# Turning q and k of six batches by crossbar DMA instead of on TensorE, with q copied by ScalarE in its own row order and k by VectorE in blocks

## The chip, the cores and the metric

The kernel runs on one core of a Trainium2 chip. The metric is the time of one execution on the device in microseconds. Executions whose time lies more than 1.5% above the fastest of the same kernel are put down as slow and left out of the ratios. A profile is one execution; its span is some 2 us shorter than the time. The granted clock is the share of TensorE's full clock that the profile records. In this kernel TensorE's results go to PSUM tiles and the other tiles lie in SBUF; a crossbar transpose (`dma_start_transpose`) is a transfer that turns a tile on its way, here from SBUF to SBUF.

## The reference

Attention over a sliding window with a bias by distance (8 batches, 8 heads, 576 rows of 64), then two matrix products with ELU between them, for 4608 tokens:

```python
rel = pos[:, None] - pos[None, :]
bias = slopes[:, None, None] * (-np.abs(rel))[None]
scores = np.where((rel >= 0) & (rel < 128), q @ k^T / 8 + bias, -1e9)
x = softmax(scores) @ v                  # then heads side by side: 4608 x 512
h = x @ w_in                             # 512 -> 2048
out = np.where(h > 0, h, np.exp(np.minimum(h, 0)) - 1) @ w_out   # 2048 -> 512
```

## The kernel before

Work is laid out in steps of about 2.1 us, 16 to a batch. In each step TensorE makes one tile of the hidden layer (`hp`), one tile of scores (`sp`), one of values (`av`) and a quarter of an output tile (`op`), each for a different stage. ScalarE takes the exponentials (`e`, `EX`) and copies finished outputs (`ob`). GpSimd clips `e`; VectorE makes `g` from `e` and `hp` (which frees the buffer of `hp`), masks `EX` and normalizes. A step s may also carry tasks, written `at(s, task)`, and the order in the program is the order on each engine.

Scores need q and k with the head's 64 dimensions on the partitions, so both are turned. A load puts rows 4p to 4p+3 of a head on partition p, so a turned tile has every fourth row side by side. The kernel before leaves q and k in that order, 32 columns to a block, and undoes it in the stores:

```python
QK = [one([128, H, 2, 640], F16, f"QK{i}") for i in range(2)]      # q and k of one batch
ps_s = ctx.enter_context(tc.tile_pool(name="ps_s", bufs=2, space=PSUM))
# ...
def load_v(b, n):                        # SyncE, four issues a block of 128 rows
    # ...
    for j in range(4):
        nc.sync.dma_start(t[32 * j:32 * j + 32, :, :],
                          v[b, :, 128 * n + j:128 * n + 128:4, :].rearrange("h p d -> p h d"))

def transposes(b, hp):                   # two heads, q and k: eight 128x128 on TensorE
    t = ps_s.tile([128, 2, 2, 4, 2, 32], F16, name="tp", tag="sps")
    # ... eight nc.tensor.transpose ...
    for odd in range(2):                 # q and k together, neighbours in runs of 32
        r = slice(64 * odd, 64 * odd + 64)
        o = QK[b % 2][0:64, 2 * hp:2 * hp + 2, :, 0:512].rearrange(
            "p h w (n a i) -> p (h w) n a i", a=2, i=32)[:, :, :, odd, :]
        i = t[r, :, :, :, :, :].rearrange("p h w n a i -> p (h w) (n a) i")
        if hp % 2:
            nc.scalar.copy(o, i)
        else:
            V.tensor_copy(o, i)
# ...
for hp in range(NP):
    at(s0 + ((5, 9, 10, 13) if b > 1 else (9, 10, 13, 14) if b else (14, 14, 15, 15))[hp],
       transposes, b + 1, hp)
# ...
for p0, rows in rows_of(512 * t + 128 * ts):          # stores of every fourth row
    nc.sync.dma_start(rows, ob[p0:p0 + rows.shape[0], :])
```

The scores share the two PSUM buffers `sps` with these turned tiles. SyncE's queue issues v's loads, the stores, and the crossbar transposes of the normalized rows (`xT<-xn`) from batch 2 on. GpSimd issues the loads of q and k.

The softmax here doesn't subtract the row's maximum and nothing guards it: scores larger than these inputs give would overflow.

## Time and profile before

| | before |
|---|---|
| time, median of 3 (lowest to highest) | 367.59 us (366.04 to 368.22) |
| span of the profile, mean clock | 363.7 us, 0.995 |
| TensorE, VectorE, ScalarE, GpSimd busy | 340.3, 243.5, 206.7, 145.7 us |
| batches 0 to 7, first step to first step (batch 0 from its step 4, the first that makes a tile of the hidden layer) | 33.4, 42.0, 38.6, 37.9, 36.8, 36.7, 36.8, 33.7 us |
| end phase, from the last batch's end to the end of the span | 51.1 us |

The views that show what bounds it are in the prediction. These are the groups on the page that the change replaces, and the granted clock of TensorE. A group line is: line, engine, operation, out<-in, shapes, count; then busy time in all and mean ns of one; then idle time just before and what ended most of it. The clock line has one digit for a fortieth of the span, in tenths.

```profile
PEclk9899999999999999999999999999999999999999
...
L322 ACT COPY QK<-tp 64x1024 f16<-64x1024 f16 x28 | 28.1, 1005 | 1.6 <-PE tp L312 1.4
...
L324 DVE COPY QK<-tp 64x1024 f16<-64x1024 f16 x28 | 19.2, 684 | 1.1 <-PE tp L312 0.8
L312 PE MATMUL tp<-ident,stq 128*128 128x128 f16 x224 | 17.1, 219 | 2.3 <-ACT QK L322 1.0
```

The reader sees 56 copies of 1024 elements a partition, spread over two engines.

### The profile page before, as it was taken

How to read it: one execution, taken by the hardware profiler on the slowest of the kernel's cores; microseconds unless marked ns; L12 is line 12 of the kernel's file. 1: busy time of each engine (PE TensorE's matmuls, PEld its weight loads, DVE VectorE, ACT ScalarE, POOL GpSimd, SP SyncE). 2: the span in 40 equal slices, each digit the busy share in tenths (PEclk: the TensorE clock that was granted, in tenths of full speed). 3: DMA queues.
4: the chain of work that ended last, by engine and by line, in shares of the span. 5: the costliest groups of instructions: out<-in, count | busy, mean ns of one | idle time of the engine just before them, and what ended most of it. 6: DMA issues, size and time to landing. Idle time of an engine off the chain costs nothing.

```text
span 363.7 us, 9613 instructions
## 1 busy us (share of the span) xinstructions
PE 340.3 (94%) x3790; PEld 251.6 (69%) x3790; DVE 243.5 (67%) x574; ACT 206.7 (57%) x349; POOL 145.7 (40%) x229
## 2 busy tenths in 40 slices
PE   6878997999979999989999999999999999999994
PEld 6766775777647667767777777777777777666651
DVE  6479889678886776666676767776776756634430
ACT  4355583666537655765566665666567565543431
POOL 9146623434314723472346334642433232233320
PEclk9899999999999999999999999999999999999999
DMA  8999999839243973497448934793631222211113
GB/s 114 198 206 119 228 107 183 151 80 155 38 103 89 133 108 84 110 128 110 98 94 127 127 88 100 120 136 82 102 84 45 52 47 45 51 43 47 29 43 73
DMA packets 81948, 37.06 MB, mean 102 GB/s; under 512 B 51952, under 2 KB 77296, under 8 KB 81904
## 3 DMA queue, kind: packets, MB, share of 16 engines
q0 software_dynamic: 34064, 15.40, 35.5%
q1 hardware_dynamic: 47840, 21.06, 25.6%
q8 instruction: 29, 0.48, 0.6%
q14 instruction: 15, 0.12, 0.1%
HBM read 36.70 MB, written 9.44 MB: 127 GB/s over the span
## 4 chain that ended last, share of the span: by engine, by line
PE 65%; DVE 14%; ACT 9%; DMA 7%; issue 3%; POOL 1%; SPq 0%; ACTq 0%; POOLq 0%
PE hp L451 27%; PE op L492 25%; PE sp L348 5%; ACT QK L322 5%; DVE VP L116 4%; DMA vs<-in_v_dram 3%; PE av L394 3%; DVE g L463 3%; ACT EX L372 2%; DVE QK L324 2%; ACT e L455 2%; DVE EX L380 2%; DMA xT<-xn 2%; DMA stq<-in_q_dram 1%; DVE xn L415 1%
## 5 line engine op out<-in xcount | busy, mean ns | idle before, releaser
L456 POOL TENSOR_SCALAR e<-e 128x512 f32<-128x512 f32 x144 | 88.6, 615 | 199.9 <-ACT e L455 199.9
L451 PE MATMUL hp<-xT,wi 128*128 128x256 f16 (+3 forms) x1536 | 150.3, 246 | 8.1 <-DVE g L463 3.6
L451 PEld LDWEIGHTS <-wi 128*128 128x128 f16 x1536 | 121.5, 98 | 49.9 <-DVE g L463 5.5
L455 ACT ACTIVATE e<-hp 128x512 f32<-128x512 f32 x144 | 86.0, 597 | 119.0 <-PE hp L451 110.0
L492 PE MATMUL op<-wo,g 128*128 128x512 f16 x576 | 146.4, 379 | 0.0
L463 DVE SCALAR_TENSOR_TENSOR g<-e,hp 128x512 f16<-128x512 f32 x144 | 98.0, 681 | 23.9 <-POOL e L456 22.7
L380 DVE TENSOR_TENSOR EX<-EX,band 128x512 f16<-128x512 f16 x112 | 49.8, 445 | 57.1 <-ACT EX L372 57.0
L372 ACT ACTIVATE EX<-sp 128x512 f16<-128x512 f32 x128 | 75.9, 593 | 13.3 <-PE sp L368 8.6
L492 PEld LDWEIGHTS <-g 128*128 128x128 f16 x576 | 51.2, 98 | 36.9
L348 PE MATMUL sp<-QK 128*128 128x128 f16 (+3 forms) x576 | 49.8, 213 | 0.0
L394 PE MATMUL av<-VP,EX 128*128 128x65 f16 x576 | 38.6, 193 | 4.3 <-DVE EX L380 2.7
L394 PEld LDWEIGHTS <-EX 128*128 128x128 f16 x576 | 31.6, 98 | 8.7 <-DVE EX L380 4.2
L415 DVE TENSOR_TENSOR xn<-av,rden 128x256 f16<-128x256 f32 x80 | 34.0, 424 | 2.8
L348 PEld LDWEIGHTS <-QK 128*128 128x128 f16 (+1 forms) x576 | 31.3, 97 | 1.0 <-issue 0.2
L496 ACT COPY ob<-op 128x512 f32<-128x512 f32 x36 | 21.1, 586 | 14.3 <-PE op L492 6.4
L322 ACT COPY QK<-tp 64x1024 f16<-64x1024 f16 x28 | 28.1, 1005 | 1.6 <-PE tp L312 1.4
L414 DVE RECIPROCAL rden<-av 128x4 f32<-128x4 f32 x80 | 14.4, 180 | 16.0 <-PE av L394 14.6
L134 POOL TENSOR_SCALAR VP<-vf 128x512 f16<-128x512 f32 (+1 forms) x25 | 19.5, 779 | 2.7 <-DMA vf<-in_v_dram 2.7
L324 DVE COPY QK<-tp 64x1024 f16<-64x1024 f16 x28 | 19.2, 684 | 1.1 <-PE tp L312 0.8
L312 PE MATMUL tp<-ident,stq 128*128 128x128 f16 x224 | 17.1, 219 | 2.3 <-ACT QK L322 1.0
L312 PEld LDWEIGHTS <-stq 128*128 128x128 f16 x224 | 13.8, 98 | 3.4 <-issue 3.2
L116 DVE COPY VP<-vs 32x512 f16<-32x512 f16 x48 | 14.9, 310 | 1.3 <-DMA vs<-in_v_dram 0.5
(70 smaller groups left out, 118.5 us busy)
## 6 DMA issues: line engine op xcount, KB each, us to landing
out_dram<-ob SPq DMA_DIRECT2D x128, 64.0 KB, 1.7
vf<-in_v_dram SPq DMA_DIRECT2D x80, 64.0 KB, 2.3
stq<-in_k_dram POOLq DMA_DIRECT2D x7, 512.0 KB, 6.4
stq<-in_q_dram POOLq DMA_DIRECT2D x7, 512.0 KB, 7.5
wi<-in_moe_w_in_dram POOLq DMA_DIRECT2D x4, 512.0 KB, 13.8
wo<-in_moe_w_out_dram POOLq DMA_DIRECT2D x4, 512.0 KB, 15.1
QK<-TQ SPq DMA_DIRECT2D x2, 576.0 KB, 8.0
vs<-in_v_dram POOLq DMA_DIRECT2D x2, 512.0 KB, 9.9
```

Source lines behind the costliest of these rows:

```text
L312: nc.tensor.transpose(t[:, g, w, :, j, :], stq[b][:, w, 2 * hp + g, 2 * j:2 * j + 2, :].rearrange("p a d -> p (a d)"), ident)
L322: nc.scalar.copy(o, i)
L348: nc.tensor.matmul(t[:, o:o + n], qk[0:r, h, 1, kc:kc + 128], qk[0:r, h, 0, qc:qc + n], start=b > 0 or o == 0, stop=b > 0)
L372: nc.scalar.activation(e[:, 0:512], t, AF.Exp, scale=0.125)
L380: V.tensor_tensor(out=e, in0=e, in1=band[:, c:c + n].unsqueeze(1).broadcast_to([128, 512 // n, n]), op=ALU.min)
L394: nc.tensor.matmul(a[:, l, :], e[:, c:c + 128], vp[:, n, h, 0:D + 1], start=st, stop=sp)
L415: V.tensor_tensor(out=xnt[b, i][:, 4 * half:4 * half + 4, :], in0=a[:, :, 0:D], in1=r.unsqueeze(2).broadcast_to([128, 4, D]), op=ALU.mult)
L451: nc.tensor.matmul(p[:, l * w + u0:l * w + u1], w_in_sb[:, c, fc * 128:(fc + 1) * 128], xT[:, c, x0:x0 + u1 - u0], start=(c == 0), stop=(c ...
L455: nc.scalar.activation(e, p, AF.Exp)
L456: nc.gpsimd.tensor_scalar(out=e, in0=e, scalar1=1.0, scalar2=0.0, op0=ALU.min, op1=ALU.max)
L463: V.scalar_tensor_tensor(out=gs[t][:, f0:f0 + nf, c0:c0 + w], in0=sh(es.pop((t, j))), scalar=1.0, in1=sh(hps.pop((t, j))), op0=ALU.subtrac ...
L492: nc.tensor.matmul(ops[t], gs[t][:, fc, ts * 128:(ts + 1) * 128], w_out_sb[:, fc, :], start=(fc == 0), stop=(fc == NFC - 1))
```

## The change

The intent is to take the transposes of batches 2 to 7 from the engine that bounds the kernel. The crossbar's output `tq` is a tile in SBUF, so it takes none of the scores' PSUM buffers. ScalarE then puts q in its own row order, by writing every fourth element, so that the output rows come in order and each store is one issue. VectorE leaves k in blocks. q and k get tiles of their own. In batches 0 and 1 TensorE still turns, but there too ScalarE copies q and VectorE copies k.

```diff
-    QK = [one([128, H, 2, 640], F16, f"QK{i}") for i in range(2)]
+    QT = [one([128, H, 576], F16, f"QT{i}") for i in range(2)]
+    KT = [one([128, H, 640], F16, f"KT{i}") for i in range(2)]
 # ... the constant rows and masks: a second set for q in its own order ...
+        def put(t, b, w, hs, c0, n):                 # batches 0 and 1, out of PSUM
+            for odd in range(2):
+                i = t[64 * odd:64 * odd + 64].rearrange("p h n a i -> p h n a i", i=32)
+                if w:
+                    # ... k: V.tensor_copy in runs of 32 ...
+                else:
+                    o = QT[b % 2][0:64, hs, c0:c0 + n].rearrange(
+                        "p h (n i a o) -> p h n a i o", a=2, o=2, i=32)[:, :, :, :, :, odd]
+                    nc.scalar.copy(o, i)
+        def cross(b, n):
+            w, hp = n // NP, n % NP
+            # ...
+            nc.sync.dma_start_transpose(
+                out=tq[b][:, w, 2 * hp:2 * hp + 2, :, :].rearrange("p h a c -> p (h a) c"),
+                in_=stq[b][:, w, 2 * hp:2 * hp + 2, :, :].rearrange("p h j d -> p (h j d)"))
+        def uncross_k(b, j):
+            # ... V.tensor_copy in runs of 32 ...
+        def uncross_q(b, n):
+            hs, j = slice(4 * (n // 4), 4 * (n // 4) + 4), n % 4
+            nc.scalar.copy(QT[b % 2][0:64, hs, 0:512].rearrange("p h (c j) -> p h c j", j=4)[:, :, :, j],
+                           tq[b][64 * (j % 2):64 * (j % 2) + 64, 0, hs, j // 2, :])
 # ...
-                for p0, rows in rows_of(512 * t + 128 * ts):
-                    nc.sync.dma_start(rows, ob[p0:p0 + rows.shape[0], :])
+                nc.sync.dma_start(out[r:r + 128, :], ob)
 # ...
+                    for n in range(8):
+                        at(s0 + (n if b > 1 else 6 + n // 2), cross, b + 1, n)
+                        at(s0 + (5 + n if b > 1 else 8 + n), uncross_q, b + 1, n)
+                        if n < 4:
+                            at(s0 + (9 + n if b > 1 else 12 + n), uncross_k, b + 1, n)
 # ...
-            at(32 + n, place_v4, 2, n)
+            at(24 + 2 * n, place_v4, 2, n)
```

## The prediction

> **What bounds the kernel now.** First the page's line of busy time:
>
> ```profile
> PE 340.3 (94%) x3790; PEld 251.6 (69%) x3790; DVE 243.5 (67%) x574; ACT 206.7 (57%) x349; POOL 145.7 (40%) x229
> ```
>
> TensorE leads, but busy time alone doesn't show that it is full, so next the busy time by stretch (length; then PE, PEld, DVE, ACT, POOL; clock, DMA share, GB/s). The first stretch is set-up and batch 0, the second the end of batch 1, the third the start of batch 2, the last one period of batch 5.
>
> ```profile
> 20.00:40.00 20.00, 15.91 (x247) 12.68 (x247) 17.84 (x52) 11.38 (x18) 10.85 (x16) 1.00 1.20 163
> ...
> 70.86:92.10 21.24, 20.45 (x293) 16.12 (x292) 16.30 (x36) 13.95 (x22) 8.06 (x13) 1.00 0.77 118
> 92.10:107.45 15.35, 12.32 (x153) 8.55 (x152) 13.00 (x38) 6.86 (x12) 3.90 (x8) 1.00 0.37 71
> ...
> 190.10:226.90 36.80, 36.33 (x377) 26.70 (x376) 25.96 (x58) 23.61 (x42) 16.68 (x26) 1.00 0.66 111
> ```
>
> In batch 0 VectorE is the fullest (17.84 of 20); at the start of batch 2 again (13.00 of 15.35, TensorE 12.32); from then on TensorE (36.33 of 36.80). The chain of waits in batch 5 shows of what a step (a sixteenth of a batch) consists:
>
> ```profile
> 214.00 0.87 PE hp L451 x8
> 214.87 0.12 PE av L394 x4
> 214.99 0.22 PE sp L348 x4
> 215.21 0.86 PE op L492 x4
> 216.08 0.87 PE hp L451 x8
> 216.95 0.12 PE av L394 x4
> 217.07 0.22 PE sp L348 x4
> 217.30 0.45 PE tp L312 x8
> ```
>
> A step is 2.08 us of gapless matmuls, and eight transposes add 0.45 us. A batch has 16 steps (33.3), 0.24 for the two steps with double av, four transpose groups (1.8), the tail's transposes (0.39): 35.7. It takes 36.8, so about 1.1 us is stall. Of that about 0.6 is at the second and fourth group, whose two ScalarE copies of 1.0 us hold a scores buffer (in the chain, ACT QK L322 twice a batch). So a transpose taken from TensorE is worth its full time there.
>
> **What the Trainium skill says.** "VectorE: DVE Perf Modes", section The three transpose paths: TensorE's transpose lands in PSUM, the crossbar DMA's in SBUF, 1309 ns for 128x128. Here the existing crossbar transposes, four such blocks each, land in 2.4 us at the median. The page gives no issue time; this trace does: 1193 ns of SyncE's queue for each of 30. Same page, section The perf-mode tier table: 16-bit copies in SBUF run up to 4x, from PSUM at most 2x. The trace agrees with the direction: 684 ns for 64x1024 from PSUM, while 32x256 and 32x512 in SBUF take about 210 and 310, which extrapolates to 0.4 to 0.5 us for 64x1024 (estimate). "ScalarE: Activation LUTs", section What ACT_TABLE_LOAD costs: a copy with immediate scale takes 186 ns + 0.833 ns an element. The trace's 128x128 copy from SBUF took 294, which is that; so 512 elements give 0.61 us (estimate). No run yet shows ScalarE writing every fourth element.
>
> **The change part by part.**
> 1. Removed: 32 transposes in each of batches 2 to 7. 6 x 4 x 0.45 = 10.8 us of TensorE, in the bounding stretch. With the stalls at the ScalarE copies, up to 6 x 2.4 = 14.4.
> 2. ScalarE: 4 copies of 1.005 (4.0 us a batch) become 8 of 0.61 (4.9). One a step fits the idle of about 1.0 us that ScalarE has before each e in most steps. Hidden.
> 3. VectorE: 4 of 0.684 (2.7) become 4 of 0.45 (1.8), and the tail's 2 of 0.417 become 4 of about 0.28 (+0.3). Even.
> 4. Set-up: VectorE gains groups(1), about 1.05 us, and loses a second subtraction (0.58), pm (0.46) and a wait for posi (1.3, early); k alone goes to it in batches 0 and 1 (+0.9 together), two split tails (+0.6). About 1 us more work where VectorE bounds; against it, q's first copy no longer waits for the second transpose group in steps 14 and 15, where ScalarE idled 0.69 twice. Net 0, give or take 1.
> 5. place_v4 of batch 2 (16 copies of 0.31, 4.8 us with their issue) moves from steps 32-35 to 24-30. Steps 32-37 then need TensorE's 12.3 instead of 15.35: -3 us. But steps 24-31 get VectorE work of 16.3 + 4.8 - 2.7 + 1.8 + 0.3 = 20.5 and still take about 21, so batch 2's own transposes gain little. Together -3.3.
> 6. SyncE's queue: 136 row stores at 0.42 become 36 whole ones, but 48 crossbar transposes at 1.2 come in, eight in the first eight steps of a batch. In that half lie already the v loads (four a pair of steps) and three turns of xn. SyncE's timeline in batch 5 of the kernel before:
>
> ```profile
> 205.82 2.72 SPq L423 DMA_TRANSPOSE xT<-xn  x2
> 208.63 2.01 SPq L126 DMA_DIRECT2D vf<-in_v_dram  x4
> 212.56 2.14 SPq L498 DMA_DIRECT2D out_dram<-ob  x4
> 214.80 1.19 SPq L423 DMA_TRANSPOSE xT<-xn  x1
> 216.09 4.45 SPq L126 DMA_DIRECT2D vf<-in_v_dram  x8
> 221.33 1.38 SPq L498 DMA_DIRECT2D out_dram<-ob  x3
> 222.83 2.34 SPq L423 DMA_TRANSPOSE xT<-xn  x1
> ```
>
> Nothing follows a transpose in less than its 1.2 us, so the issue blocks the queue. Put the new order end to end, counted from the batch's first step (205.38 here). Ahead of cross 7, the last quarter of k, lie four turns of xn at 1.3 with the gap behind them (5.2), seven crosses at 1.25 (8.7), three groups of v loads at 2.05 (6.2) and two stores at 0.55 (1.1). The first turn finds its xn ready at 0.2, and after it the queue doesn't run empty: cross 7 starts at 0.2 + 5.2 + 8.7 + 6.2 + 1.1 = 21.4 and lands 2.4 later, at 23.8. VectorE reaches the first copy of k after the cut of step 9: 9 x 2.08 + 0.2 (the first step is longer) + 2.6 = 21.5. So it stands 2.3 us. Behind the copy lies the elu of step 9, which frees the buffer of the hidden tile of step 11, due at 11 x 2.08 + 0.2 = 23.1. With 0.45 for the copy and 0.65 for the elu: 23.8 + 0.45 + 0.65 - 23.1 = **1.8 us of TensorE stall per batch**. Some issues here take 1.05 more (the 2.34 above), others' gaps are shorter, so 1.2 to 2.7, 1.9 in the middle.
>
> **Sum.** Batches 2 to 6 (which turn 3 to 7): 5 x (2.4 - 1.9) = 2.5. Batch 2's start: 3.3. Set-up 0. The last store: one issue instead of four, 1.2 less, with a longer landing: 0.5. Total about 6.3: 367.6 - 6.3 = 361.3, say 361.
>
> **Rivals.**
> A. The transfers are hidden. If SyncE runs far enough ahead or the copy of k is not missed, all 2.4 us a batch stay: 5 x 2.4 + 3.3 + 0.5 = 15.8, 352 us. For it: SyncE waits 149 us in total for ob, so over a whole batch it has room (about 28 us of work in 35), and the writer put two steps between the last cross and its use. Against: the bunching above.
> B. ScalarE becomes the bound in steps 5 to 12: exp, e, a quarter of ob and the copy are 0.5 + 0.5 + 0.12 + 0.52 = 1.65 of 2.08. If writing every fourth element costs 1.0 instead of 0.61, it is 2.0 and every store step slips, about 1 us a batch: 366.
> C. DMA contention. Landings of turns beside q and k loads took 4.6 to 6.4 instead of 2.4; the crosses come before those loads, mostly beside v loads, where 2.4 to 3.6 was seen. If crosses took 5, stall grows by 2.6 a batch: 374. Also late v loads would hold GpSimd's cast, and with it e.
> D. "SBUF — State Buffer", section two separate sides: a VectorE copy in a two-port mode locks GpSimd out for its whole length. Four copies of 0.45 a batch against e's min of 0.61; TensorE copies from PSUM did not do that. At worst 1 us a batch; the casts of v (4 times 0.31 in a row) show e's min at 0.72 instead of 0.61, so less.
>
> **Range and chances.** A gives 352, B 366, both of C's ends near 370; my sum 361, which is 1.8% under the median before. The 2% line is 360.2, within the error of a stall of 1.2 to 2.7 times five (7 us). So 353.5 to 368, chances 0.46 faster, 0.48 same, 0.06 slower.
>
> **What would show it.** tp L312 falls from 224 to 32 transposes. ScalarE's new copies at 0.61 mean, VectorE's at 0.45. A wait of VectorE's first k copy on the DMA that fills tq, about 2 us in each of batches 2 to 6, and after it hidden tiles waiting for elu; SyncE without a gap from the batch's start to cross 7, about 21 us. Steps 32 to 37 in 12 us. If that wait is absent, rival A holds and I am wrong by 9 us; if copies of q take 1 us, B; if crosses land in 5, C.

## The result

The changed kernel is correct and slower: 402.81 us median of four runs (397.02 to 408.65), of which two, 397.02 and 400.44, count as fast; the kernel before took 367.9 beside it. A ratio in this document is the mean time of one kernel's fast runs over that of the other's of the same rounds, so not quite the ratio of the medians. Here it is 1.083 (95% interval 1.069 to 1.098). The other two, 405.19 and 408.65, are left out by the 1.5% rule, though their clocks (0.953 and 0.941, against 0.949 and 0.952) set them little apart; with all four the ratio would be 1.094. The profile is of the run of 400.44 us.

The page after, in the lines that answer to those of before:

```profile
PE 343.8 (86%) x3598; PEld 249.6 (63%) x3598; DVE 244.0 (61%) x601; ACT 252.7 (63%) x381; POOL 145.2 (36%) x230
...
PEclk9696988999699998999899999999996999999999
...
L353 ACT COPY QT<-tq 64x512 f16<-64x512 f16 x48 | 64.4, 1341 | 1.1
...
L345 DVE COPY KT<-tq 64x1024 f16<-64x1024 f16 x24 | 10.5, 436 | 21.7 <-DMA tq<-stq 21.3
...
L303 ACT COPY QT<-tp 64x512 f16<-64x512 f16 x12 | 15.5, 1295 | 6.0 <-DVE KT L298 5.1
```

TensorE has 192 matmuls fewer and yet 3.5 us more busy time, with its clock falling in several slices (mean 0.949). The prediction gave those transposes 10.8 us, so some 14 us more went into the rest of its work (an estimate from these numbers). VectorE's k copies take what was predicted, 436 ns, but wait 21 us for the crossbar. ScalarE's q copies take 1341 ns from SBUF and 1295 from PSUM, twice the predicted 610, and ScalarE's busy time rises by 46 us.

The time from first step to first step shows that the loss lies in every stage but the last batch, which turns nothing, and the end. Here `start` ends where step 4 of batch 0 begins.

| us | start | b0 | b1 | b2 | b3 | b4 | b5 | b6 | b7 | end |
|---|---|---|---|---|---|---|---|---|---|---|
| before | 16.7 | 33.4 | 42.0 | 38.6 | 37.9 | 36.8 | 36.7 | 36.8 | 33.7 | 51.1 |
| after | 20.0 | 39.9 | 53.0 | 41.6 | 41.9 | 40.0 | 37.1 | 41.1 | 33.7 | 50.3 |

**Batches 0 and 1.** ScalarE's timeline (start, duration, engine and line, operation, count; in brackets the idle time before and its releaser) has in steps 14 and 15 of batch 0:

```profile
51.04 5.22 ACT L303 COPY QT<-tp 64x512 f16<-64x512 f16 x4 [0.73 <-PE tp L327]
...
57.91 5.25 ACT L303 COPY QT<-tp 64x512 f16<-64x512 f16 x4 [0.53 <-DVE KT L298]
```

Before, ScalarE had two copies of 1.0 us (2.03) in each of these places. While it holds the turned tiles, the scores have no PSUM buffer. In batch 1 a second thing comes in. These lines are VectorE's, TensorE's in the step after it, and TensorE's one step later:

```profile
102.73 0.42 DVE L345 COPY KT<-tq 64x1024 f16<-64x1024 f16 x1 [7.07 <-DMA tq<-stq]
...
105.12 1.89 PE L480 MATMUL hp<-xT,wi 128*128 128x128 f16 x16 [7.07 <-DVE g L492]
...
109.13 1.06 PE L480 MATMUL hp<-xT,wi 128*128 128x128 f16 x16
```

VectorE stands at the first k copy until the last crossbar transpose has landed, 7.07 us. Behind that copy lie four copies that place v (1.18 us) and the `g` that frees a hidden buffer, so TensorE stands as long. The 16 matmuls after it take 1.89 us; the next 16, 4 us later, take 1.06.

**Batch 4**, in which the clock stayed at 1.00, can be accounted for nearly in full. Its steps of 2.1 us are longer in three places. The lines are from the timelines of ScalarE, TensorE, VectorE and GpSimd:

```profile
211.42 1.34 ACT L353 COPY QT<-tq 64x512 f16<-64x512 f16 x1
...
213.24 1.02 PE L506 MATMUL op<-wo,g 128*128 128x512 f16 x4 [0.72 <-ACT ob L510]
...
221.77 0.53 DVE L345 COPY KT<-tq 64x1024 f16<-64x1024 f16 x1 [2.58 <-DMA tq<-stq]
...
222.94 1.03 PE L480 MATMUL hp<-xT,wi 128*128 128x256 f16 x8 [2.32 <-DVE g L492]
...
228.86 0.62 POOL L136 TENSOR_SCALAR VP<-vf 128x512 f16<-128x512 f32 x1 [3.55 <-DMA vf<-in_v_dram]
...
230.82 0.69 DVE L492 SCALAR_TENSOR_TENSOR g<-e,hp 128x512 f16<-128x512 f32 x1 [2.55 <-POOL e L485]
...
231.56 1.05 PE L480 MATMUL hp<-xT,wi 128*128 128x256 f16 x8 [2.19 <-DVE g L492]
```

First, in the step with an output store, the q copy of 1.34 us delays ScalarE's `ob` copy and TensorE waits 0.7 us for it (step of 3.0 us, +0.9). Second, the k copy waits 2.58 us for the crossbar, and TensorE 2.32 for what lies behind it (+2.6). Third, v's load of 222.07 lands 6.65 us later, beside the 512 KB load of k issued at 221.13; GpSimd's cast waits 3.55 us for it and holds `e`, VectorE waits for `e`, and TensorE for VectorE, 2.19 us (+2.4). Together +5.9; the removed transposes are -2.4 by the prediction; so 36.8 becomes 40.3, and 40.0 was measured.

SyncE's queue in that batch, which starts at 196.40 (first part and last):

```profile
196.82 1.22 SPq L339 DMA_TRANSPOSE tq<-stq  x1
198.46 2.05 SPq L452 DMA_TRANSPOSE xT<-xn  x1
200.56 1.26 SPq L339 DMA_TRANSPOSE tq<-stq  x1
201.92 2.01 SPq L128 DMA_DIRECT2D vf<-in_v_dram  x4
203.97 1.19 SPq L339 DMA_TRANSPOSE tq<-stq  x1
...
219.15 1.26 SPq L339 DMA_TRANSPOSE tq<-stq  x1
220.51 2.01 SPq L128 DMA_DIRECT2D vf<-in_v_dram  x4
```

It has no gap worth naming until the last crossbar of k at 219.15, 22.75 us after the batch's start; it landed 2.49 us later.

### The profile page after: what moved, and what is told of

Same layout as the page of the kernel before. It is cut to its first block, busy times and chain, and to the rows that moved or that the text cites. A ratio compares the mean times of both kernels' runs of the same rounds, so it can differ in the third digit from the quotient of the medians.

```text
span 398.6 us, 9247 instructions
## 1 busy us (share of the span) xinstructions
PE 343.8 (86%) x3598; PEld 249.6 (63%) x3598; DVE 244.0 (61%) x601; ACT 252.7 (63%) x381; POOL 145.2 (36%) x230
## 4 chain that ended last, share of the span: by engine, by line
PE 54%; DMA 12%; ACT 12%; DVE 10%; SPq 5%; issue 5%; POOL 1%; ACTq 0%; DVEq 0%; POOLq 0%
PE hp L480 23%; PE op L506 20%; DMA tq<-stq 5%; PE sp L377 5%; DMA vf<-in_v_dram 4%; ACT QT L353 4%; ACT QT L303 3%; DVE g L492 3%; PE av L423 3%; ACT EX L401 3%; DMA xT<-xn 3%; DVE VP L118 2%; SPq L339 2%; ACT e L484 2%; SPq L452 2%
## 5 line engine op out<-in xcount | busy, mean ns | idle before, releaser
L480 PE MATMUL hp<-xT,wi 128*128 128x256 f16 (+3 forms) x1536 | 157.3, 253 | 32.7 <-DVE g L492 24.1
L480 PEld LDWEIGHTS <-wi 128*128 128x128 f16 x1536 | 126.2, 101 | 76.7 <-issue 19.1
L484 ACT ACTIVATE e<-hp 128x512 f32<-128x512 f32 x144 | 88.2, 612 | 108.9 <-PE hp L480 100.9
L506 PE MATMUL op<-wo,g 128*128 128x512 f16 x576 | 149.0, 384 | 4.0 <-ACT ob L510 4.0
L353 ACT COPY QT<-tq 64x512 f16<-64x512 f16 x48 | 64.4, 1341 | 1.1
L377 PE MATMUL sp<-QT,KT 128*128 128x128 f16 (+3 forms) x576 | 51.7, 219 | 4.5 <-ACT QT L303 4.5
L377 PEld LDWEIGHTS <-KT 128*128 128x128 f16 (+1 forms) x576 | 33.0, 100 | 5.7 <-issue 4.5
L510 ACT COPY ob<-op 128x512 f32<-128x512 f32 x36 | 22.2, 616 | 12.9 <-PE op L506 11.7
L345 DVE COPY KT<-tq 64x1024 f16<-64x1024 f16 x24 | 10.5, 436 | 21.7 <-DMA tq<-stq 21.3
L303 ACT COPY QT<-tp 64x512 f16<-64x512 f16 x12 | 15.5, 1295 | 6.0 <-DVE KT L298 5.1
L118 DVE COPY VP<-vs 32x512 f16<-32x512 f16 x48 | 16.7, 348 | 0.8
L519 PE MATMUL spare<-ident 128*128 128x128 f16 x94 | 8.9, 269 | 1.6 <-DVE ident L179 1.6
## 6 DMA issues: line engine op xcount, KB each, us to landing
wi<-in_moe_w_in_dram POOLq DMA_DIRECT2D x4, 512.0 KB, 12.3
```

The source lines that it names most:

```text
L353: nc.scalar.copy(QT[b % 2][0:64, hs, 0:512].rearrange("p h (c j) -> p h c j", j=4)[:, :, :, j], tq[b][64 * (j % 2):64 * (j % 2) + 64, 0, h ...
L377: nc.tensor.matmul(t[:, o:o + n], kt[0:r, h, kc:kc + 128], qt[0:r, h, qc:qc + n], start=b > 0 or o == 0, stop=b > 0)
L480: nc.tensor.matmul(p[:, l * w + u0:l * w + u1], w_in_sb[:, c, fc * 128:(fc + 1) * 128], xT[:, c, x0:x0 + u1 - u0], start=(c == 0), stop=(c ...
L484: nc.scalar.activation(e, p, AF.Exp)
L506: nc.tensor.matmul(ops[t], gs[t][:, fc, ts * 128:(ts + 1) * 128], w_out_sb[:, fc, :], start=(fc == 0), stop=(fc == NFC - 1))
```

## The experiments

Four causes were in question: **the step** (ScalarE's write of every fourth element), **the queue** (SyncE's crowded order makes the last crossbar late, and then it meets the loads), **the split** (two engines read one PSUM tile), and **batch 1's crowd** of transfers. The runs marked wrong leave rows in wrong places to remove a cost alone. (The reference computed with q's rows shuffled changes by only 1.2%, so the comparison says little about q's order in the correct runs.) The wrong runs are e1, e3, e5, e6, e7, e9, e10, e13, e14 and e15.

### The step, measured by itself

Run e4_probe is the kernel before with copies of 64x512 appended at its end, four of each kind:

```diff
+        for _ in range(4):
+            nc.scalar.copy(at_step(4), src)      # and at_step(1), (2), (8); runs of 32; out of PSUM
+        for _ in range(4):
+            V.tensor_copy(at_step(4), src)       # and at_step(1), (2)
```

> Edit: the kernel before, with copies of 64x512 fp16 appended after its last step, four of each kind, to measure the disputed cost alone: ScalarE from SBUF to neighbouring elements, to runs of 32, to every second, fourth and eighth element, from PSUM to neighbouring and to every fourth, and a read of every fourth element written densely; VectorE from SBUF to neighbouring, every second and every fourth, and from PSUM to every fourth. Theory 1: ScalarE writes neighbours and runs of 32 at 0.61 us and every fourth at about 1.34; a stepped read costs nothing. Rival for the 1.34: not the step but reading tq from other partitions or contention with the stream; then every fourth takes about 0.61 here. VectorE: 0.28 for neighbours, 0.6 to 0.7 for steps.

Its groups by form, in the order: neighbours, every second, every fourth, every eighth element written by ScalarE; neighbours and every fourth by VectorE.

```profile
L611 ACT COPY xT<-wi 64x512 f16<-64x512 f16 x4 | 2.5, 616 | 0.1
...
L615 ACT COPY xT<-wi 64x512 f16<-64x512 f16 x4 | 3.0, 756 | 0.1
...
L617 ACT COPY xT<-wi 64x512 f16<-64x512 f16 x4 | 5.3, 1320 | 0.1
...
L619 ACT COPY xT<-wi 64x512 f16<-64x512 f16 x4 | 9.8, 2450 | 0.1
...
L627 DVE COPY xT<-wi 64x512 f16<-64x512 f16 x4 | 1.2, 290 | 41.4 <-ACT xT L625 41.3
...
L631 DVE COPY xT<-wi 64x512 f16<-64x512 f16 x4 | 2.9, 729 | 0.1
```

Runs of 32 took 616 as well, a stepped read with a dense write 636, and from PSUM it was 582 for neighbours and 1287 for every fourth. So the stepped write alone doubles the copy, with the other engines done. The cause of the long copy is shown; what it costs the kernel is another question.

### The step taken away in the kernel

Run e1_q_dense writes q in runs of 32 (wrong):

```diff
-            nc.scalar.copy(QT[b % 2][0:64, hs, 0:512].rearrange("p h (c j) -> p h c j", j=4)[:, :, :, j],
+            nc.scalar.copy(QT[b % 2][0:64, hs, 0:512].rearrange(
+                "p h (n j i) -> p h n j i", j=4, i=32)[:, :, :, j, :],
                 # ... and the same in put ...
```

> Edit: every ScalarE copy of q writes runs of 32 neighbouring elements (the block order that k has) instead of every fourth element; same sizes, same sources, nothing else. The result is wrong on purpose (q's rows lie in another order than the masks say). Theory 1 (the stepped write of ScalarE, 1.34 us and 1.30 us instead of 0.61 and 0.58, is the main loss, through batches 0 and 1 above all): means fall to about 0.61 from SBUF and 0.58 from PSUM, steps 4 to 16 take about 33 us again instead of 39.9, and the whole about 362 us, my prediction's sum. Rival (SyncE's crowded queue makes the k transposes late, VectorE and then TensorE stand still, and TensorE's clock falls): the time stays over 385 us, VectorE's wait on tq at 20 us or more.

Measured: 394.04 us, ratio to before 1.066 (1.057 to 1.075). The copies fell to 617 ns, but only some 6 us came back, in the start and in batch 0 (17.2 and 35.9 us). A miss for the first theory; the time and VectorE's wait are those that the expectation named for its rival, the queue. The waits (engine, what for, us in all, times, longest) grew:

```profile
DVE KT L346 <- DMA tq<-stq: 34.7, 6, 8.2
```

In batch 5 of this run the last crossbar was issued right behind the 512 KB load of k and landed after 6.24 us instead of 2.5; in 9.8 us TensorE worked 2.2. The load went out 23.3 us after that batch's start, 24.7 in the changed kernel: with faster copies its step comes sooner and meets the late crossbar.

### The k copies later, the loads later

Run e2_k_late moves VectorE's k copies three steps back, e3_dense_late does that and writes q densely, e5_dense_loads writes densely and issues the loads of q and k at steps 12 and 14 instead of 12 and 10, e6_dense_loads_late does all three.

```diff
-                            at(s0 + (9 + n if b > 1 else 12 + n), uncross_k, b + 1, n)
+                            at(s0 + 12 + n, uncross_k, b + 1, n)                  # late
-                for i, w in enumerate((1, 0)):
-                    at(s0 + 10 + 2 * i, load_qk, b + 2, w)
+                for i, w in enumerate((0, 1)):
+                    at(s0 + 12 + 2 * i, load_qk, b + 2, w)                        # loads
```

> Edit: VectorE's four copies of k out of tq move from steps 9 to 12 of a batch to steps 12 to 15 (for batches 3 to 7; batch 2's stay). Nothing else; the result is right. Theory 1: VectorE's wait on tq in batches 3 to 7 (about 14 us of the 21.3) goes, but ScalarE still takes 1.34 us a copy, so about 390 us, 2 to 3 per cent under the changed kernel. Rival: 375 us or less, and the granted clock near 0.99.

> Edit: both of the above together (wrong result on purpose). If the two losses are separate and are all there is: the transposes' full worth is left, about 352 us, which is my prediction's rival A. If a third cost is there (q's loads, v's loads behind the crossbar transposes, the split tails): 358 us or more.

> Edit: as e1 (q written in runs of 32, wrong result on purpose), and the loads of q and k two batches ahead move from steps 10 and 12 of a batch (k first) to steps 12 and 14 (q first, since the crosses take q first). Theory 3 (SyncE's queue runs late, so that the last crosses of k fall behind the 512 KB k load issued by GpSimd at step 10, and land in 6 us instead of 2.5; VectorE waits 8 us, TensorE with it, and its clock drops): the last cross lands in about 2.5 us again, VectorE's wait falls from 34.7 us to about 12 (the 2.3 a batch of my prediction), the clock rises to 0.98 or more, and the time falls from 394 to about 370. Rival 3b (crossbar transposes and loads share the DMA engines at all times, so landings stay at 5 to 7 us wherever the loads lie): 388 or more.

> Edit: as e5, and the copies of k at steps 12 to 15 as in e2. Theory 3: nothing waits on tq in batches 3 to 7 any more and GpSimd's casts of v don't wait over 5 us in total; about 360, a gain over the kernel before. Rival 3b: 388 or more, with the wait moved to the casts of v, as in e3.

| run | median us | ratio to before (95%) | VectorE's wait for the crossbar | GpSimd's wait for v |
|---|---|---|---|---|
| after | 402.81 | 1.083 (1.069 to 1.098) | 21.3 | 9.7 |
| e2_k_late | 406.01 | 1.105 (1.098 to 1.112) | 9.5 | 24.5 |
| e3_dense_late | 395.73 | 1.073 (1.064 to 1.082) | 9.8 | 39.6 |
| e5_dense_loads | 388.72 | 1.059 (1.051 to 1.067) | 26.9 | 8.4 |
| e6_dense_loads_late | 375.35 | 1.022 (1.014 to 1.029) | 7.5 | 18.9 |

All four are misses, e6 the least. In e2 and e3 the wait for the crossbar fell to one place near batch 1's end, and the same time was lost at v's cast, whose load stands behind the crossbars in SyncE's queue and beside k's load. e5 brought the landing back to 2.5 us in batches 2 to 5, but the last crossbar is still issued 22.7 to 24.5 us after the start of batches 4 to 6. Only together (e6) do they help. The queue itself must be relieved.

### The queue relieved

Run e7_dense_v_one writes q densely and loads v's blocks with one issue instead of four (wrong, relative error 0.98). The trace shows one issue of 128 rows at 0.53 us, as long as one of 32 rows. Run e14_step_v_one has that edit alone, on the kernel after.

```diff
-            for j in range(4):
-                nc.sync.dma_start(
-                    t[32 * j:32 * j + 32, :, :],
-                    v[b, :, 128 * n + j:128 * n + 128:4, :].rearrange("h p d -> p h d"))
+            nc.sync.dma_start(t, v[b, :, 128 * n:128 * n + 128, :].rearrange("h p d -> p h d"))
```

> Edit: as e1, and each block of v is loaded by one issue of 128 rows instead of four of 32 (same bytes and descriptors; v's rows come in natural order, so the result is wrong on purpose, twice). It takes about 1.0 to 1.4 us of SyncE's queue from each of four v groups a batch and touches no load of q or k. Theory 3: cross 7 is issued 3 to 4 us earlier, before the k load, and lands in 2.5; VectorE's wait falls under 10 us; about 368. Rival 3b: the landings stay long, 388 or more. Rival 3c (the issue time goes with the number of descriptors, so one issue of 128 rows takes as long as four): no change against e1.

> The kernel after with nothing changed but v's loads: one issue a block of 128 rows instead of four (v's rows then lie wrong, on purpose). With dense copies the same edit took 394.0 to 367.7 us. If SyncE's issues in the first half of a batch are the root of the late crossbar whatever ScalarE does, it removes as much here: some 377 us, with VectorE's wait for the crossbar down from 21 to 9 us or less, all in batch 1 to 2. If ScalarE's stepped copies hold the batches back anyway, it stays at 390 or more.

| ratio to before | v in four issues | v in one issue |
|---|---|---|
| q stepped | 1.083 (after) | 1.054 (1.049 to 1.059; e14, 386.12 us) |
| q dense | 1.066 (e1) | 0.999 (0.993 to 1.005; e7, 367.69 us) |

The waits of e7 for the crossbar, all that is left being at batch 1 and the start of 2:

```profile
DVE KT L343 <- DMA tq<-stq: 8.8, 4, 7.6
```

In batch 4 of e7 the last crossbar is issued 18.8 us after the batch's start (22.75 after the change), and batches 4 to 6 take 34.2 us, 2.6 less than before the change. That is the gain that the transposes were worth. The table also shows that the two causes aren't a sum: alone the dense write gives 1.7 points of ratio and the relieved queue 2.9, together 8.4 (e1's interval overlaps those of after and e14; e7's is clear of all three). In e14 VectorE's wait for the crossbar fell from 21.3 to 7.4 us, and batches 4 to 6 take 36.4: against e7 the stepped copies cost 2.2 us a batch there. I had expected 377 or at least 390 for e14, and it lies between: both causes act.

### The split

Runs e8_step_no_crossbar and e9_dense_no_crossbar let TensorE turn all batches, with k copied by VectorE and q by ScalarE, stepped and dense; e13_one_engine_a_tile is e9 with both copies of a tile on one engine, in turn.

```diff
-                    for n in range(8):
-                        # ... cross, uncross_q, uncross_k ...
+                for hp in range(NP):
+                    at(s0 + ((5, 9, 10, 13) if b > 1 else (9, 10, 13, 14) if b else (14, 14, 15, 15))[hp],
+                       transposes, b + 1, hp)
 # e13, in put:
+            copy = nc.scalar.copy if turned[0] % 2 else V.tensor_copy
+            turned[0] += w == 0
```

> Edit: the changed kernel with TensorE's transposes for every batch again, so no crossbar transposes of q and k; ScalarE's stepped copies from PSUM, whole-row stores, split tiles and set-up as changed. The stepped write alone: batches 0 and 1 take 17 us more than before (as in the changed kernel), the later batches about 1 us more each because ScalarE has 6 us more work of 37: 385 to 392. If stepped writes matter only together with the crossbar: 375 or less.

> The kernel after with TensorE turning every batch, as in the run without the crossbar (440.7 us), but q's copies of ScalarE written in neighbouring runs of 32 (0.58 us each instead of 1.3; values of q in wrong places on purpose). It separates the two things that the 440.7 us mixed. Theory 'the step': ScalarE's 4 copies a tile shrink from some 5.2 to 2.3 us, the scores' two PSUM buffers come free about as early as in the kernel before, and the time falls to 368 to 378 us. Rival 'the split': that q's copies on ScalarE wait for VectorE's k copies of the same PSUM tile (39 us of such waits in that run) holds the buffers as well, and the time stays at 395 or more.

> The kernel after with TensorE turning all batches and dense copies (387.6 us), but all four copies of a PSUM tile now on one engine, VectorE and ScalarE tile by tile as in the kernel before, instead of k on VectorE and q on ScalarE (q still in blocks, wrong on purpose). Theory 'the split': ScalarE's q copies no longer wait for VectorE's k copies of the same tile (30 us of such waits), the PSUM buffers of the scores come free earlier, and the time falls to 366 to 374 us, batches 2 to 6 to 37 to 38 us each from 40. Rival: the loss is from the separate q and k tiles (four copies of 512 a tile instead of two of 1024) or from the set-up, and it stays above 380.

| run | median us | ratio to before (95%) | batches 3 to 6 |
|---|---|---|---|
| e8_step_no_crossbar | 440.71 | 1.197 (1.191 to 1.203) | 47.5 to 47.7 us |
| e9_dense_no_crossbar | 387.57 | 1.056 (1.050 to 1.062) | 40.2 to 40.9 |
| e13_one_engine_a_tile | 374.66 | 1.021 (1.015 to 1.026) | 38.1 to 38.2 |

e8 was a large miss. In e9 the largest new wait is this one:

```profile
ACT QT L303 <- DVE KT L298: 30.1, 19, 5.5
```

ScalarE's q copy waits for VectorE's k copies of the same PSUM tile. VectorE comes to them late, and ScalarE is then held with `EX` and `e` behind it. In e13 this wait isn't there, and 13 us are won. So the split costs by itself: some 2 us a batch here. What it costs with stepped copies isn't shown: e8 has both, and no run has the step without the split. The changed kernel has the split in batches 0 and 1 only, and its cost there was not measured alone. Against the kernel before, e13 still loses 7.7 us in the start and batches 0 and 1 and 1.3 to 1.5 in each of batches 4 to 6, and gains 1.2 in batch 2. It has four copies of 512 to a tile for two of 1024, and the changed set-up; I did not take these apart further.

### Batch 1's crowd

In every run above with crossbars batch 1 took 48 to 56 us (42.0 before). Run e15_v_one_batch1 is e7 (wrong too) with batch 1's eight crossbars one a step from its step 3, not two a step from step 6, with the constant rows filled before them, and with batch 2's q loaded ahead of its k:

```diff
-                        at(s0 + (n if b > 1 else 6 + n // 2), cross, b + 1, n)
+                        at(s0 + (n if b > 1 else 3 + n), cross, b + 1, n)
-        at(22, fill, 0)
-        at(22, fill_k, 0)
+        at(17, fill, 0)
+        at(18, fill_k, 0)
 # ...
-            at(16 + i, load_qk, 2, w)
+            at(16 + i, load_qk, 2, 1 - w)
```

> The run with dense copies and v in one issue (367.7 us, batch 1 at 51.1 us; result still wrong on purpose) with batch 1's crossbar transposes sent one a step from step 3 of the batch on, and the constant rows filled before them instead of in their midst. Theory: eight transposes in four steps behind the fills and beside batch 3's loads are what makes batch 1 8 to 9 us longer than in the kernel before: batch 1 becomes 42 to 44 us and the time 358 to 361. Rival: batch 1 is long for its set-up work on VectorE and GpSimd, and stays above 48 us.

Measured: 362.46 us, ratio 0.988 (0.982 to 0.994). Batch 1 took 46.6 us instead of 51.1, half of what I expected. The three edits together are shown as a cause of that half; which of them did it is open. Batch 3 took 40.6 us in e15 and 37.7 in e7: in both TensorE waits there once, 3.35 and 3.23 us, for a crossbar transpose of `xT` that landed 8 us after its issue, and in e15 its clock then fell.

### The clock

Run e10_dense_loads_warm puts 48 matmuls on nothing (2.7 us at full clock) into each of five batches of e5, just ahead of the stall.

> The run with dense q copies and later loads (388.7 us) with 48 useless matmuls of 128x128 in step 10 of batches 2 to 6, where TensorE is about to stand still for some 4 us behind the wait for the last k crossbar: 2.7 us of work at full clock, so the idle time shrinks below 2 us and the end of the stall doesn't move. If a part of the loss is TensorE's halved clock after an idle stretch, the added work makes the kernel faster: 376 to 384 us, mean granted clock up from 0.973, and the steps after the stall at 0.9 to 1.06 us per 16 matmuls instead of up to 1.9. If the stall alone is the loss, it stays within 2 us of 388.7 or becomes slower by up to the added 13 us.

Measured: 385.94 us, ratio 1.052 (1.047 to 1.056), against 1.059 (1.051 to 1.067) for e5; the intervals overlap, and the profile's mean clock is 0.973 in both. Added work of 13 us did not lengthen the kernel, so most of it lay in the stalls.

The sum leaves the question open, but single batches answer it. These are the first hidden matmuls after batch 6's stall in the changed kernel, in e5 and in e10:

```profile
301.01 1.86 PE L480 MATMUL hp<-xT,wi 128*128 128x256 f16 x8 [3.35 <-DVE g L492]
...
284.92 1.86 PE L483 MATMUL hp<-xT,wi 128*128 128x256 f16 x8 [3.98 <-DVE g L495]
...
289.42 1.03 PE L483 MATMUL hp<-xT,wi 128*128 128x256 f16 x8 [1.17 <-DVE g L495]
```

In batches 4 to 6 of e5 TensorE stands for 3.9 to 4.9 us, and the two steps after the stalled one take 5.6 to 6.8 us together. In e10, with 1.2 to 1.9 us of idle time left, they take 4.2. So the colder clock costs 1.4 to 2.6 us a batch there beyond the stall; e10's sum hides it because batches 1 and 3 of its profile were 3.5 and 3.1 us longer than e5's, batch 1 with the same program. In batch 3 the clock went the other way: it held after 3.2 us of idle time in e5 and fell after 2.4 in e10. In batch 6 of the changed kernel these two steps take 6.8 us: 2.6 of its loss are the clock's.

### A correct kernel without the four causes

Runs e11 to e17 are correct. Batch 0 stays in blocks, with its four stores split. From batch 1 on q, k and v are loaded with row 128 n + p on partition p, so that turned rows come in order, all copies write neighbours, v needs one issue a block, and stores are whole. Each PSUM tile is read by one engine.

```diff
-        nc.gpsimd.dma_start(
-            stq[b][:, w, h0:h1, :, :].rearrange("p h j d -> p h (j d)"),
-            (q, k)[w][b, h0:h1, 0:512, :].rearrange("h (p j) d -> p h (j d)", j=4))
+        for j in js:
+            nc.gpsimd.dma_start(
+                stq[b][:, w, h0:h1, j, :],
+                (q, k)[w][b, h0:h1, 128 * j:128 * j + 128, :].rearrange("h p d -> p h d"))
 # ...
+            nc.scalar.copy(QT[b % 2][0:64, hs, 128 * j:128 * j + 128],
+                           tq[b][64 * (j % 2):64 * (j % 2) + 64, 0, hs, j // 2, :])
 # ... batches 1 and 2: v cast by the load straight into VP; a second band for rows in order ...
 # e16: the four loads of q and of k one or two a step, not four in one; the second band in steps 13 to 15
 # e17: batch 1's q loads at steps 7 to 10, ahead of the last output weights and v;
 #      batch 2's crossbars at steps 23 to 28, its q copies from step 26
```

> A correct kernel made of what the experiments found. Batch 0 stays in blocks for q, k and v (its four stores are split again). From batch 1 on q, k and v are loaded with row 128 n + p on partition p, so that both engines' copies write neighbours and v needs one issue a block on SyncE and no placing copies by VectorE; every PSUM tile of batches 0 and 1 is read by one engine; q and k loads two ahead are issued at steps 12 and 14; batch 1 sends one crossbar transpose a step from step 3 on, with the fills of the constant rows before them instead of in their midst. The run with v in one issue took 367.7 us; batch 1 should lose its 8 to 9 us (51 to some 43 us), the start some 4: 350 to 358 us. Rival: the q and k loads now move 256-byte rows instead of 1 KB, land much later than 7 us, and the waits for the crossbar come back: 365 us or more.

> The same with VectorE's four k copies three steps later (steps 12 to 15 of a batch). If the landing of the last crossbar is still near step 9 or 10, this removes the remaining wait and takes 345 to 352 us, 3 to 8 less than the run with them at steps 9 to 12. If v's casts on GpSimd wait for their loads instead, as in the run with late copies and stepped writes, it is no faster or slower.

> The correct kernel with rows in order from batch 1 on (373.4 us), its q and k loads spread to one or two issues a step, so that GpSimd isn't held for 3.6 us by four issues in steps 12 and 14, and the second band and the groups of rows computed in steps 8 and 13 to 15 instead of all in 8 to 10. In the run before, VectorE waited 46.6 us for GpSimd's e against 22.7; batches 2 to 6 took 35.5 to 36.9 us, of which the last and first step lose 2 to 3. Expected: batches 2 to 6 at 34 to 35 us, batch 0 at 36 to 38, in all 352 to 360 us. Rival: the 256-byte rows slow the first loads and batch 0 stays above 40 us: 362 or more.

> The correct kernel with rows in order and spread loads (367.1 us), whose batches 3 to 6 took 34.1 to 34.4 us (before: 36.7 to 37.9), but batch 0 43.5 and batch 1 46.5. Two waits there made most of it: TensorE's transposes of step 14 for batch 1's q loads (step of 9.3 us), and ScalarE's first q copy of batch 2 for its crossbar (8.5 us), both transfers that came late in a crowd of others. Here batch 1's q loads go out at steps 7 to 10 ahead of the last output weights and of v, and batch 2's crossbars start when its loads have landed, with its q copies two steps later. Expected: batch 0 at 36 to 38 us, batch 1 at 38 to 41, in all 350 to 357 us, faster than before by 3 to 4%. Rival: the transfers of the first 100 us fill the DMA engines whatever their order, the waits only move, and it stays at 362 or more.

| run | median us | ratio to before (95%) | b0 | b1 | b4 |
|---|---|---|---|---|---|
| e11_rows_in_order | 373.45 | 1.018 (1.014 to 1.022) | 41.3 | 45.0 | 36.9 |
| e12_rows_in_order_late | 373.32 | 1.021 (1.016 to 1.026) | 41.7 | 43.1 | 36.8 |
| e16_rows_spread | 367.08 | 1.001 (0.998 to 1.004) | 43.5 | 46.5 | 34.1 |
| e17_rows_tuned | 358.33 | 0.978 (0.973 to 0.982) | 36.1 | 42.3 | 34.6 |

e11 and e12 missed: a load is now four issues of 0.9 us, and GpSimd, held 3.6 us, gave `e` late (VectorE waited 46.6 us for it, 22.7 before). Spread out (e16) they cost nothing in batches 3 to 6, but batches 0 and 1 had steps of 9 to 10 us at two late transfers. Ordered anew (e17), these went. e17 is 2.2% faster than the kernel before; the interval reaches from 1.8 to 2.7%, so it is faster, but not surely by 2%. Which part of its layout gives how much was not separated; it also has 16 of VectorE's copies that place v, where the changed kernel has 48. It came out 1 us above the range that I expected. Its busy line shows TensorE as full as before the change, with less to do:

```profile
PE 331.9 (94%) x3598; PEld 243.7 (69%) x3598; DVE 237.0 (67%) x576; ACT 212.0 (60%) x381; POOL 188.6 (53%) x278
```

## Why the prediction was wrong

**Step 1, the transposes removed, was right.** 192 of 224 are gone, and where nothing else interferes a batch becomes 34.2 us from 36.8 (e7, e17 nearly): 2.6 against the predicted 2.4.

**Step 2 failed: "ScalarE: 4 copies of 1.005 (4.0 us a batch) become 8 of 0.61 (4.9). ... Hidden."** They took 1.34, so 10.7 us a batch. The formula had been checked on a copy to neighbours, and the text itself said that no run had shown the stepped write. Rival B took it up, but at 1.0 us and at "about 1 us a batch"; the two runs with one issue of v give 2.2.

**Step 4 failed: "Net 0, give or take 1."** The start and batch 0 became 9.8 us longer. The stepped copies hold the scores' buffers there. The four profiles with stepped copies in this part (after, e2, e8, e14) took 59.9 to 62.5 us for it, the seven with dense ones (e1, e3, e5, e6, e7, e9, e10) 50.9 to 54.6, and the kernel before 50.1 and, in e4's profile, 52.4. So the step makes some 9 us, and what is left is not clear of the scatter. The claim that q's first copy would wait less was wrong in kind: the last profile line of the page after shows it waiting for VectorE's k copies, and e9 against e13 shows what such a split costs elsewhere. Batch 1 became 11.0 us longer; 7 of these are the stall at the crossbar (step 6).

**Step 5 was half right.** Steps 32 to 37 took 12.9 us, from 15.4 (predicted 12.3). Steps 24 to 31, said to "still take about 21", took 30.1, with the 7 us at the crossbar in them.

**Step 6 was right for the wait that it worked out.** In batch 4: issue of the last crossbar at 22.75 (predicted 21.4), landing 2.49 (2.4), VectorE's wait 2.58 (2.3), TensorE's stall 2.32 (1.8). It failed as the whole of the queue's cost. It took the landing as 2.4 for all: in batch 1 the last four crossbars, beside the 512 KB loads of k and q, took 6.9 to 7.25. And it followed only the crossbar in the queue, not v's load behind it, which costs another 2.4 us in batch 4. Rival C had such a landing, "late v loads would hold GpSimd's cast" included, and then set it aside because the crossbars come before those loads (its "near 370" in the range is also not the 374 that it had worked out). A queue that runs late moves them to the loads.

**The sum** therefore missed some 20 us in the start and batches 0 and 1, and lost some 15 in batches 2 to 6, where 5.8 had been expected as gain (2.5, and 3.3 at batch 2's start). Rival D did not show: of three of GpSimd's clips beside a k copy two took 0.61 us and one 0.74.

**A term was missing: the clock.** The Trainium skill, "TensorE: Matmul & The Clock Gate", section What's actually happening, has TensorE fall to half clock after at least one idle window of about 3.4 us, in windows that run freely. The trace agrees on the half: after 7.07 us of idle 16 matmuls took 1.89 us, after 3.35 us eight took 1.86. It shows no sharp line at 3.4 us: after 2.53 us in batch 3 of the changed kernel eight took 1.71, and after 3.54 us in batch 6 of e1 eight took 1.03. The 14 us or so by which TensorE's remaining work took longer are an upper bound of what the clock cost in all, since a part may be hidden; batch 6's 2.6 us are not hidden (see The clock).

## What to carry to other kernels

Before work is moved to another engine, measure the new operation in the form it will have there: the step of its write doubled a copy that a formula had right for neighbours. Ask of a queue not only when the moved transfer comes, but what stands behind it, and what load it meets if it is late; a wait pushed off one engine came back on the next one until the queue itself got fewer issues. A stall of TensorE can cost more than its length: where the clock fell after one, the next two steps took 1.4 to 2.6 us more. Read a PSUM tile with one engine, and look for the layout in which loads, copies and stores are all in order: here loading row 128 n + p took away the stepped write, three of four issues, and the split stores at once.

## What the Trainium skill lacked or had wrong

- "SBUF — State Buffer", section Door 1: The DMA port swizzle, says: "So how far you can stride for free depends on dtype: 4 fp32, 8 bf16, 16 int8." For ScalarE's writes the runs show no free step with 16-bit elements: 616 ns for neighbours, 756 for every second, 1320 for every fourth, 2450 for every eighth; VectorE took 290 for neighbours, 448 for every second and 729 for every fourth. "ScalarE: Activation LUTs", section What ACT_TABLE_LOAD costs, gives 186 ns and 0.833 ns an element, so 613 for 512 elements (an estimate from its figures), which the dense copy meets (616), and says nothing of a stepped output.
- "DMA: Bandwidth & Descriptors", section DMA Transpose (X-bar), gives no time that an issue holds the queue (1.19 to 1.26 us here for four blocks of 128x128) and no landing beside other transfers (2.4 to 2.6 us for most, 6.2 to 8.8 beside 512 KB loads). Elsewhere that page compares sequencer cycles per issue with those of trn3's faster path, but gives none for a tile of this kind. Nor does it say that an ordinary issue of 128 rows takes as long as one of 32 (0.53 us in e7; four in 2.01 in the changed kernel).
- No page that I read has the cost of two engines reading one PSUM tile: 13 us over 32 tiles between e9 and e13.
